# A planned DeltaNet and SwiGLU kernel: two early weight loads tied to the first solve, and a planner that replays a list of key changes

## The chip, the cores and the metric

The kernel runs on one core of one Trainium2 chip. The metric is the device time of one execution in microseconds; the median of the runs shown is what counts. A profiled execution is a single one; its span runs from its first to its last instruction.

## The reference

There are 4 batches of 8 heads, 768 tokens and head size 48, and a feed-forward of 384 to 1536 to 384 over 3072 tokens, all in float32 on the chip (the weights and inputs arrive as 64-bit numbers).

```python
k_n = k / (np.linalg.norm(k, axis=-1, keepdims=True) + 1e-06)
for t in range(S):
    y[:, :, t] = np.einsum('bhd,bhde->bhe', q[:, :, t], state)
    v_old = np.einsum('bhde,bhd->bhe', state, kt)
    state = state + bt[:, :, :, None] * np.einsum('bhd,bhe->bhde', kt, vt - v_old)
# x: y as (tokens, 384)
xn = x / rms * rms_g
g = xn @ w_gate
out = (silu(g) * (xn @ w_val)) @ w_out
```

## The kernel before

**The work.** The sequence is cut into 12 chunks of 64 tokens. For each chunk and head the recurrence over 64 tokens becomes a triangular system. The kernel computes the score matrix of the keys with themselves (`scores`, matmuls at L671), inverts a triangular matrix per head, applies the inverse to v minus the state's prediction, adds the part of the output that comes from within the chunk, and updates the state. The output of a chunk (4 batches x 64 tokens = 256 rows) is normalised, turned around, and goes through the feed-forward.

- Chunks 0 and 1 are solved by blocks of 16: `prep16` inverts the 16-blocks on DVE (L835, L841), and `recur` couples them by three rounds of small products (`couple`, L1202) with a subtraction on DVE (L1250) and copies on ACT (L1244) between the rounds. `first_rows` is L1190, the coupling matrices are L888 (copied by ACT at L893), the gather of the blocks is L780.
- Later chunks use blocks of 32: `prep` sends the scores through DRAM into another layout (`dkk`, `at`), inverts on DVE (L991, L997), sends the result back (`dx`, `dxt`, `m1bd`, `x2bd`, `mt`), and two merges on TensorE (`merge1` L1046 with its copy L1055, `merge2` L1066) fill the off-diagonal block. `recur` then does the products with the state (L1105), with the inverse (L1176), and L1212/L1284 for output and state.
- `norms` gives the key norms (L692 to L699), `qpart` the scores of q with k (L671, masked by DVE at L715), L1315 to L1370 the output's RMS and its transposition into `xf` or, for chunk 1, `xp1` (the profile's `xp`). ACT scales it with `g_sb` at L1370.
- The feed-forward of chunks 0 and 1 is plain (`ffn_plain`: up products L1433, ACT L1440, DVE L1441 writes `hf`, down products L1415), in two halves of the hidden width. The other ten use a fast product scheme with fewer multiplications (`ffn`: L1526, L1536, L1538, L1542, L1543, and `down`: L1583, L1575, L1588, L1592).
- `weights(n0, n1)` loads the feed-forward's weights in 18 pieces of 768 KB, numbered 0 to 17: gate, value, gate, value, out and so on. Each is converted from 64-bit numbers by ACT (L588) and four DVE operations (L576, L579, L584, L608). The buffers are three slices of `more`, but loads 3 and 4 use the two halves of `hf` (`early`), which the feed-forward doesn't use yet. All of these DMAs are issued by SP (L454).

**The order.** Nothing is scheduled by the compiler. Every step is given to a `Plan` with its engine, an estimated duration, a due time, and keys for what it reads and writes. `Plan.run` makes a list schedule (`forward`), takes the latest possible starts from it (`backward`) as the next keys, perturbs them a little, and repeats this 150 times; the plan with the earliest modelled end is emitted. Each engine executes its own list in that order, and waits on semaphores for what it reads. A step that SP, ACT or POOL waits for holds all that stands behind it on that engine. Where the plan has TensorE idle in the first 70 us, products with the identity matrix are put in as fillers (L1692). `RELEASE` gives the earliest planned time of each weight load; it puts no wait into the program.

The sequence in which steps are given to the plan (which fixes dependencies and the late steps' due times) is the loop at the end of the function: for each chunk `recur`, then the next chunk's `prep`, then the later weights, loads, norms and `qpart`, then the feed-forward.

Of the kernel before, what the change touches and what calls it, by code (L numbers as in the profile page):

```python
# [19 lines left out]
W = 32  # L20
# [5 lines left out]
ROUNDS, SEEDS = 150, (53,)  # L26
# [3 lines left out]
JKQ, JMR, JSC = 3, 99, 99  # L30
EARLYN = (3, 4)
RELEASE = (4.7, 10.0, 13.0, 16.0, 30.0, 33.0, 36.0)
# [39 lines left out]
class Plan:  # L72
# [198 lines left out]

    def run(self, free, filler=None, until=0.0):
        self.first_priorities()
        first = [op.key for op in self.ops]
        best = None
        self.ends = []
        for seed, k in itertools.product(SEEDS, range(ROUNDS)):
            if not k:
                rng = random.Random(seed)
                for op, key in zip(self.ops, first):  # L280
                    op.key = key
            order = self.forward([t for t, _ in free], until if filler else 0.0)
            if order is None:
                continue
            self.ends.append(self.end)
            if best is None or self.end < best[0]:
                best = self.end, [(op, op.start) for op in order]
            self.backward()
            for op in self.ops:
                if op.first:  # L290
                    op.key = op.n - 2000.0
                op.key += SHAKE * (k % 3) * rng.uniform(-1.0, 1.0)
        self.end = best[0]
        pe = 0.0
        free = list(free)
        for op, s in best[1]:
            op.start = s
            for g in op.acquire:
                if g.t is None:
                    g.t = free.pop(0)[1]  # L300
            if filler and op.eng == "PE":
                if s < until:
                    filler(fillers(pe, s))
                pe = s + op.dur
            op.fn()
            for g in op.release:
                g.left -= 1
                if not g.left:
                    free.append((s + op.dur + 0.1, g.t))
                    free.sort(key=lambda x: x[0])  # L310
# [3 lines left out]
def kernel(  # L314
# [298 lines left out]


# [46 lines left out]

    def scores(kt_, rhs, pr, r, w):

        ps = [Group(), Group()]

        def sc():
            for u in range(8):
                for d in range(2):
                    for g in range(2):
                        s, c_ = slice(64 * d, 64 * d + 64), slice(64 * g, 64 * g + 64)  # L670
                        nc.tensor.matmul(ps[d].t[c_, 64 * u : 64 * u + 64], kt_[s, u, c_], rhs[s, u, c_])  # L671

        P.rows = 64
        P.add("PE", 0.99, sc, pr, r=r, w=ps + w, ps=ps, size=128)
        P.rows = 128
        return ps
# [26 lines left out]
    def qpart(c):  # L703
        pr = (13.0, 41.0)[c] if c < 2 else due(c, 50)
        i2 = c % NKQ
        qk = [("qt", hv) for hv in range(2)]
        if c < 2:
            turn(q2, qt, qk, q2k + ["q2p"], pr, False)
        else:
            square_turn(qt, qk, pr)  # L710
        ptall = [("pt", d) for d in range(2)]
        ps = scores(kt[i2], qt, pr, qk + [("kt", i2, hv) for hv in range(2)], ptall)
        for d in range(2):
            dst = pt[:, d:16:2]
            P.add("DVE", 0.72, lambda d=d, dst=dst: nc.vector.tensor_tensor(  # L715
                out=dst, in0=heads(ps[d]), in1=mask_p[:, None, :].to_broadcast([128, 8, C]), op=ALU.mult,
            ), pr, r=[ps[d], "mask"], w=[("pt", d)], last=ps[d])
# [15 lines left out]
    def prep16(c):  # L733
# [147 lines left out]
        for h in range(2):  # L881
            ps = Group()

            def coupling(h=h, ps=ps):
                for z_ in range(8):
                    for g in range(2):
                        rows, x_ = slice(64 * g, 64 * g + 64), 8 * (z_ // 4) + 4 * h + z_ % 4
                        nc.tensor.matmul(ps.t[rows, 64 * z_ : 64 * z_ + 64], under[rows, x_], dg[c][rows, 8 * h + z_])  # L888

            P.rows = 64  # L890
            P.add("PE", 1.04, coupling, pi, r=[("dg", c, h), "under"] + (kkall if c else mtkeys()), w=[ps, ("ET", h)], ps=ps, size=64)
            P.rows = 128
            P.add("ACT", A(512), lambda h=h, ps=ps: nc.scalar.copy(et[:, 8 * h : 8 * h + 8], ps.t.rearrange("p (z t) -> p z t", t=C)), pi, r=[ps], w=[("ET", h)], last=ps)  # L893

    def prep(c):
        pr = due(c, 110)
        pn = due(c, 125)
        pd = pr + 1
        pi = due(c, 80)
        i2, ikq, ikk = c % 2, c % NKQ, c % 2  # L900
        kn = k2[c % NK]
        kd = kn[:, :, 0:D]
        kkeys = kkeys_(c)
        ktk = [("kt", ikq, hv) for hv in range(2)]

        fast = c < 4
        eng, e_ = (nc.vector, "DVE") if fast else (nc.gpsimd, "POOL")
        kkd = lambda d: [("kka", ikk // 2, d), ("kkb", ikk, d)]
        kkall = kkd(0) + kkd(1)
        kp = [("k2p", c % NK)]  # L910
        P.add("POOL", 1.6, lambda: nc.gpsimd.tensor_tensor(
            out=kd, in0=kd, in1=krec[i2][:, :, None].to_broadcast([128, 16, D]), op=ALU.mult,
        ), pn, r=[("krec", i2)], w=kkeys)
        if c < KSQ:
            turn(kn, kt[ikq], ktk, kkeys + kp, pr, False)
        else:
            dma(dsq, kn.rearrange("p x e -> p (x e)"), pn, r=kkeys + kp, w=["dsq"], dur=0.6, work=1.4)
# [5 lines left out]
        ps = scores(kt[ikq], kt[ikq], pr, ktk, kkall)  # L923
        for d in range(2):
            dst = kk[ikk][:, :, d:16:2]
            src = lambda d=d, ps=ps: ps[d].t.rearrange("p (u i t) -> p i u t", u=8, i=2)
            P.add("ACT", A(512), lambda dst=dst, f=src: nc.scalar.mul(dst, f(), -1.0), pr, r=[ps[d]], w=kkd(d), last=ps[d])

        dk = dkk[c % 2]
        for g in range(2):  # L930
            for i in range(2):
                r0 = 64 * g + W * i
                src = kk[ikk][r0 : r0 + W, i]
                kbkeys = [(("kka", ikk // 2, d), ("kkb", ikk, d))[i] for d in range(2)]
                dma(dk[i, g].rearrange("x j t -> j x t"), src, pd, r=kbkeys, w=[("dkk", c % 2, g, i)], work=0.5, dur=0.55)
# [105 lines left out]
        ps1 = Group()  # L1041

        def merge1():
            for b in range(B):
                for y_ in range(4):
                    nc.tensor.matmul(  # L1046
                        ps1.t[W * y_ : W * y_ + W, 64 * b : 64 * b + 64],
                        kk[ikk][:, 1, 4 * b + y_],
                        m1bd[:, 4 * b + y_].rearrange("p g s -> p (g s)"),
                    )  # L1050

        P.rows = 32
        P.add("PE", 0.5, merge1, pi, r=[("kkb", ikk, d) for d in range(2)] + [("m1bd", g, bb) for g in range(2) for bb in range(2)], w=[ps1, ("yn", 0)], ps=ps1, size=64)
        P.rows = 128
# [4 lines left out]
        ps2 = Group()  # L1059

        def merge2():
            for p in range(2):
                for g in range(2):
                    for bb in range(2):
                        r0 = 64 * bb + W * g
                        nc.tensor.matmul(  # L1066
                            ps2.t[r0 : r0 + W, 128 * p : 128 * p + 128],
                            zz[:, 2 * bb + p, g],
                            x2bd[:, 4 * g + 2 * bb + p].rearrange("p y t -> p (y t)"),
                        )  # L1070

        P.rows = 32
        P.add("PE", 0.5, merge2, pi, r=[("yn", 0)] + [("x2bd", y_) for y_ in range(4)], w=[ps2] + [("mt", 0, 2, bb, g) for bb in range(2) for g in range(2)], ps=ps2, size=32)
        P.rows = 128
# [6 lines left out]


    def recur(c):
# [11 lines left out]
        if c:  # L1095
# [26 lines left out]
            if c == 1:  # L1122
                scale_v(c, pr)
            P.rows = 64
            if c < JKQ:
                P.add("PE", 0.98, lambda: (on_state if c > 1 else on_state_rows)(kt[ikq], psk), pr, r=ktk + sk, w=psk + rk, ps=psk, size=128)
            else:

                def both_states():
                    on_state(kt[ikq], psk)  # L1130
                    on_state(qt, psq)

                P.add("PE", 1.96, both_states, pr, r=ktk + qk + sk, w=psk + psq + rk, ps=psk + psq, size=256)
# [118 lines left out]
        for h in halves:  # L1252
            gu = groups(psu, h) if c else [psu[0, h[0]]]
            P.rows = 64
            if c > 1:
# [5 lines left out]
            if c > 1:  # L1261
                continue
            ek = [("ET", p) for p in h]
# [372 lines left out]
    weights(0, 9)  # L1636
# [9 lines left out]
    for c in range(NCH):  # L1646
        for part_ in (recur, prep):
            P.late = c + (part_ is prep) > 1
            if part_ is prep:
                P.slack, P.lead = 0.0 if c < 1 else 0.2, 1000.0  # L1650
                if c + 1 < NCH:
                    (prep if c else prep16)(c + 1)
            else:
                P.slack, P.lead, P.first = 0.0 if c < 1 else 0.1, 1000.0, c == 0
                recur(c)
                P.first = False
# [5 lines left out]
        if c + 2 < NCH:  # L1662
            load(c + 2, "k")
            norms(c + 2)
# [63 lines left out]
```

## Time and profile before

| | us |
|---|---|
| Median of 3 runs (lowest, highest) | 676.82 (675.74, 678.0) |
| Profiled execution | 677.15 |
| Its span | 675.4 |
| TensorE busy | 660.1 |
| VectorE (DVE) busy | 547.8 |
| ScalarE (ACT) busy | 300.5 |
| GpSimd (POOL) busy | 133.6 |

The profile's page names engines as PE (TensorE's matmuls), PEld (its weight loads), DVE, ACT, POOL and SP. A line such as L1526 is the line of the kernel before. [...] "Idle before" with an arrow is the time that an engine sat idle ahead of an instruction, and what released it. The granted clock is the share of full speed that TensorE was given: its mean over the span is 0.995.

### The profile page before, as it was taken

To read this page: it belongs to the slowest core of one execution; us is meant where nothing else is said; L and a number is where in the kernel's file an instruction comes from. 1 tells how busy PE (TensorE), PEld (TensorE's weight loads), DVE (VectorE), ACT (ScalarE), POOL (GpSimd) and SP (SyncE) were. 2 spreads that over 40 slices of the span, in tenths; PEclk is the share of its full clock that TensorE was granted. 3 is DMA by queue.
4 is the path that set the end of the run, shared out by engine and by line. 5 is a ranking of instruction groups with operands and counts; after the bars stand their busy time and mean duration, and the time that the engine had idled before them with its cause. 6 is when DMAs were issued, how large, how long until landed. Compare 5 with 4: busy or idle time off the path is not lost.

```text
span 675.4 us, 23509 instructions
## 1 busy us (share of the span) xinstructions
PE 660.1 (98%) x10068; PEld 611.6 (91%) x10068; DVE 547.8 (81%) x1154; ACT 300.5 (44%) x693; POOL 133.6 (20%) x141
## 2 busy tenths in 40 slices
PE   8899999999999999999999999999999999999997
PEld 6787877778899999999999999999989999999997
DVE  6989999999699599599699599599699689467472
ACT  7565462244256355354444453454354354353341
POOL 4112031030321330331421331330331111000000
PEclk9989999999999999999999999999999999999999
DMA  9868985516114535445455635546535622402101
GB/s 141 257 110 197 240 197 109 91 26 107 36 34 71 89 77 94 77 97 92 69 138 74 115 94 85 104 106 100 90 76 104 113 48 58 72 2 48 24 1 24
DMA packets 266329, 62.32 MB, mean 92 GB/s; under 512 B 253168, under 2 KB 258288, under 8 KB 266224
## 3 DMA queue, kind: packets, MB, share of 16 engines
q1 hardware_dynamic: 263104, 60.22, 46.1%
q8 instruction: 79, 1.29, 0.8%
q10 hardware_dynamic: 3120, 0.59, 0.7%
q14 instruction: 26, 0.21, 0.1%
HBM read 44.25 MB, written 16.52 MB: 90 GB/s over the span
## 4 chain that ended last, share of the span: by engine, by line
PE 63%; DVE 15%; SPq 8%; DMA 7%; issue 3%; ACT 2%; POOL 1%; DVEq 0%; POOLq 0%; ACTq 0%
PE bank L1526 30%; PE bank L1583 16%; SPq L454 8%; PE bank L1433 5%; PE bank L1415 3%; DVE acc L997 2%; DMA more<-in_moe_w_val_dram 2%; DVE tmp L1536 2%; PE bank L1105 2%; DVE acc L991 2%; PE bank L671 2%; PE bank L1202 1%; DMA q<-dsq 1%; PE bank L1176 1%; PE bank L1212 1%
## 5 line engine op out<-in xcount | busy, mean ns | idle before, releaser
L1526 PE MATMUL bank<-xf,w_in 128*128 128x128 f32 x1440 | 181.0, 277 | 0.1
L1526 PEld LDWEIGHTS bank<-xf,w_in 128*128 128x128 f32 x1440 | 170.0, 192 | 3.2 <-issue 1.0
L1536 DVE TENSOR_TENSOR tmp<-tmp,bank 128x512 f32<-128x512 f32 x180 | 120.5, 680 | 39.6 <-PE bank L1526 27.3
L1526 PE MATMUL bank<-xf,more 128*128 128x128 f32 x960 | 124.2, 277 | 0.7 <-DVE tmp L1536 0.5
L1526 PEld LDWEIGHTS bank<-xf,more 128*128 128x128 f32 x960 | 114.9, 192 | 2.9 <-DVE tmp L1536 1.4
L1538 ACT COPY tmp<-bank 128x512 f32<-128x512 f32 x120 | 69.0, 585 | 78.3 <-PE bank L1526 62.4
L1542 ACT ACTIVATE tmp<-tmp 128x256 f32<-128x256 f32 x120 | 49.9, 418 | 100.0 <-DVE tmp L1536 99.9
L997 DVE TENSOR_REDUCE acc<-acc 128x30 f32<-128x90 f32 (+4 forms) x150 | 70.9, 473 | 5.2
L695 POOL TENSOR_TENSOR knrm<-ksum,half 128x16 f32<-128x16 f32 x12 | 35.7, 2979 | 152.7 <-DVE ksum L694 152.7
L1583 PE MATMUL bank<-wo_sb,hf 128*128 128x192 f32 x360 | 64.5, 329 | 0.0
L1583 PEld LDWEIGHTS bank<-wo_sb,hf 128*128 128x128 f32 x360 | 58.2, 190 | 0.7 <-issue 0.2
L991 DVE TENSOR_TENSOR acc<-acc,at 128x60 f32<-128x60 f32 (+4 forms) x150 | 51.3, 342 | 8.6 <-POOL at L974 3.3
L1543 DVE TENSOR_TENSOR hf<-tmp 128x256 f32<-128x256 f32 x120 | 50.2, 436 | 5.9 <-ACT tmp L1542 5.3
L944 POOL TENSOR_TENSOR at<-at,beta_b 128x1024 f32<-128x1024 f32 x8 | 18.9, 2358 | 129.7 <-DMA at<-dkk 99.3
L1017 POOL COPY acc<-acc 128x128 f32<-128x128 f32 x40 | 17.6, 469 | 91.5 <-DVE acc L997 91.1
L1415 PE MATMUL bank<-wo_sb,hf 128*128 128x384 f32 x96 | 34.0, 489 | 0.8 <-DVE hf L1441 0.8
L1433 PE MATMUL bank<-xf,w_in 128*128 128x256 f32 x144 | 34.6, 386 | 0.0
L1592 DVE TENSOR_TENSOR tmp<-tmp,bank 128x192 f32<-128x192 f32 x30 | 10.5, 350 | 28.5 <-PE bank L1583 28.5
L1433 PE MATMUL bank<-xp,w_in 128*128 128x256 f32 x144 | 32.8, 380 | 0.4 <-DVE hf L1441 0.4
L1433 PEld LDWEIGHTS bank<-xp,w_in 128*128 128x128 f32 x144 | 27.0, 190 | 5.4 <-DVE hf L1441 0.6
L1433 PEld LDWEIGHTS bank<-xf,w_in 128*128 128x128 f32 x144 | 26.5, 190 | 5.0
L1588 ACT COPY tmp<-bank 128x192 f32<-128x192 f32 x30 | 9.6, 321 | 42.8 <-PE bank L1583 38.4
(192 smaller groups left out, 1021.0 us busy)
## 6 DMA issues: line engine op xcount, KB each, us to landing
at<-dkk SPq DMA_DIRECT2D x20, 256.0 KB, 3.9
more<-in_moe_w_gate_dram SPq DMA_DIRECT2D x6, 768.0 KB, 9.6
vt<-in_v_dram SPq DMA_DIRECT2D x24, 192.0 KB, 4.6
out_dram<-tmp SPq DMA_DIRECT2D x48, 96.0 KB, 2.2
k<-in_k_dram SPq DMA_DIRECT2D x23, 192.0 KB, 3.9
more<-in_moe_w_val_dram SPq DMA_DIRECT2D x5, 768.0 KB, 6.2
more<-in_moe_w_out_dram SPq DMA_DIRECT2D x5, 768.0 KB, 5.7
dyn<-yn SPq DMA_DIRECT2D x16, 192.0 KB, 1.9
```

The costliest lines, as they stand in the source:

```text
L454: op = P.add(eng, dur, lambda: queue.dma_start(out=dst, in_=src), prio, r, w, lat=0.7)
L695: P.add("POOL", 2.95, lambda: nc.gpsimd.tensor_tensor(out=knrm[i2], in0=ksum[i2], in1=half, op=ALU.pow), pn, r=[("ksum", i2), "half"], w=[ ...
L991: nc.vector.tensor_tensor(out=acc[:, 1:3, 0:n, j + 2 : W].rearrange("p a i t -> p i a t"), in0=acc[:, old, 0:n, j : j + 2, None].to_broadc ...
L997: nc.vector.tensor_reduce(out=acc[:, new, 0:n, j + 2 : W], in_=acc[:, lo : lo + 3, 0:n, j + 2 : W].rearrange("p a i t -> p i t a"), axis=A ...
L1415: nc.tensor.matmul(po[p].t[:, 0:DM], hf[:, spot(f), 128 * p : 128 * p + 128], wo_sb[:, spot(f)], start=(f == f0), stop=(f == f1 - 1), skip ...
L1433: nc.tensor.matmul(ps.t[:, TOK * side : TOK * side + TOK], w_in[:, side, h_, 3 * t + i_, n : n + 128], x_[:, 2 * t : 2 * t + 2].rearrange( ...
L1526: nc.tensor.matmul(g.t[:, 128 * z : 128 * z + 128], fac[:, side, 128 * f : 128 * f + 128], xf[:, xs], start=(begin and z == 0), stop=False ...
L1536: P.add("DVE", V(512), lambda t=t, g=g: nc.vector.tensor_tensor(out=t, in0=t, in1=g.t, op=ALU.add), -1, r=[g], w=[tk], last=g)
L1538: P.add("ACT", A(512), lambda t=t, g=g: nc.scalar.copy(t, g.t), -1, r=[g], w=[tk], last=g)
L1542: P.add("ACT", A(256), lambda t=t: nc.scalar.activation(out=t[:, 0:256], in_=t[:, 0:256], func=ACTF.Silu), -1, w=[tk])
L1543: P.add("DVE", V(256), lambda t=t, f0=f0, p=p: nc.vector.tensor_tensor(out=hf[:, spot(f0) : spot(f0) + 2, 128 * p : 128 * p + 128], in0=t[ ...
L1583: nc.tensor.matmul(g.t[:, 0:192], a_[:, f], b_[:, f], start=(begin and f == 0), stop=(f == 5), skip_group_check=True)
```

## The change

- **Holds.** A new helper `hold(i, ...)` adds a one-element POOL copy into half `i` of `hf`. Loads 3 and 4 go into these halves, so that each now waits for its copy. The first copy reads the second coupling matrix of chunk 0 after ACT wrote it (L893); the second reads `u` of the second half of chunk 0 after ACT's copy (L1244). The loads 0 to 2 are given to the plan first; loads 3 to 8 after `recur(0)`. `RELEASE` gets one more 16.0 in place of 36.0.
- **Planner.** 150 rounds with seed 53 become 3 rounds with seed 23, followed by 61 listed seeds. Each seed stands for one draw in `shake`: it adds random amounts to the keys of some steps (1, 4 or 20% of those whose start lies in a stretch), or starts from `backward` anew. The earliest modelled end is kept, as before.
- **Stages.** `prep` is split into `kscores` (scores, their copy and the way to DRAM) and `invert`. `merge1` is given to the plan in `qpart`, ahead of the scores of q, and `merge2` in `recur`. Further branches, which would join merges and scores with other products into one step, are behind `JQM`, `JTM` and `JMK`; all three are 99, and with 12 chunks none of them is taken.

No other operation is added or removed, and no size changes. The core of the diff:

```diff
-ROUNDS, SEEDS = 150, (53,)
+ROUNDS, MOVES = (3, 23), (3000241, 3001356,
...
-RELEASE = (4.7, 10.0, 13.0, 16.0, 30.0, 33.0, 36.0)
+RELEASE = (4.7, 10.0, 13.0, 16.0, 16.0, 30.0, 33.0)
...
+    def shake(self, state):
+        def draw():
+            nonlocal state
+            state = (state * 6364136223846793005 + 1442695040888963407) % 2**64
+            return (state >> 11) * 2.0**-53
+        for _ in range(4):
+            draw()
+        kind, a, b, c = draw(), draw(), draw(), draw()
+        if kind < 0.03:
+            self.backward()
+            self.reorder()
+            for op in self.ops:
+                op.key += 0.24 * a * (draw() * 2.0 - 1.0)
+            return
+        share = 0.01 if a < 0.33 else 0.04 if a < 0.66 else 0.2
+        far = 0.5 if b < 0.33 else 2.0 if b < 0.66 else 6.0
+        wide = 2000.0 if kind < 0.4 else 30.0 if kind < 0.7 else 8.0
+        t = -1000.0 if kind < 0.4 else c * self.end
+        for op in self.ops:
+            x = draw()
+            if t <= op.start < t + wide and x < share:
+                op.key += far * (draw() * 2.0 - 1.0)
...
+        seed, rounds = ROUNDS
+        for k in range(rounds + len(MOVES)):
...
+            if k >= rounds - 1:
+                if k < rounds + len(MOVES) - 1:
+                    self.shake(MOVES[k - rounds + 1])
+                continue
             self.backward()
+            self.reorder()
...
+    def hold(i, src, keys):
+        first, P.first = P.first, False
+        P.add("POOL", 0.15, lambda: nc.gpsimd.tensor_copy(out=hf[:, 6 * i, 0:1], in_=src), 0, r=keys, w=[("hf", f, p_) for f in range(6 * i, 6 * i + 6) for p_ in range(2)])
+        P.first = first
...
+        if c < JQM:
+            if c > 1:
+                merge1(c)
+            ps = scores(kt[i2], qt, pr, qk + [("kt", i2, hv) for hv in range(2)], ptall)
...
+            if c == 0 and h:
+                hold(0, et[:, 8, 0:1], [("ET", 1)])
...
             if c == 1:
                 scale_v(c, pr)
+            elif c < JTM:
+                merge2(c)
...
+            if c == 0 and h[0]:
+                hold(1, u_[:, 4, 0:1], uk(h))
...
-    weights(0, 9)
+    weights(0, 3)
...
+        recur(c)
+        P.first = False
+        if c == 0:
+            P.lead = 0.0
+            weights(3, 9)
...
+        if c == 0:
+            prep16(1)
+        elif c + 1 < NCH:
+            if c < JMK:
+                kscores(c + 1)
+            invert(c + 1)
```

## The prediction

> **What bounds the kernel now.** I read the page's shares and slices first, then the busy time by stretches, then TensorE's instructions in order of time, then the chain of waits.
>
> ```profile
> PE 660.1 (98%) x10068; PEld 611.6 (91%) x10068; DVE 547.8 (81%) x1154; ACT 300.5 (44%) x693; POOL 133.6 (20%) x141
> PE   8899999999999999999999999999999999999997
> DVE  6989999999699599599699599599699689467472
> PEclk9989999999999999999999999999999999999999
> ```
>
> TensorE (PE) is busy in 98% of the span. But PE's busy time up to about 54 us holds filler products (L1692), and "busy" hides slow ones.
>
> ```profile
> 0.00:30.00 30.00, 25.38 (x512) 20.08 (x514) 22.83 (x67) 19.47 (x34) 9.74 (x17) 1.00 0.90 194
> 30.00:70.00 40.00, 38.42 (x758) 32.81 (x755) 37.09 (x73) 22.94 (x54) 6.49 (x4) 0.91 0.81 169
> 70.00:112.00 42.00, 40.10 (x725) 31.83 (x721) 40.55 (x79) 17.57 (x38) 8.43 (x8) 1.00 0.73 174
> 112.00:200.00 88.00, 88.00 (x1023) 72.91 (x1026) 79.24 (x160) 32.64 (x78) 16.57 (x14) 1.00 0.38 70
> ```
>
> The columns are PE, PEld, DVE, ACT, POOL, the granted clock, the DMA share and GB/s. From 112 us on PE has no slack: over 112 to 671.4 us it is busy 556.2 of 559.4 us, idle 3.2. From 30 to 112 us DVE is nearly full (77.6 of 82). So the end is PE's fixed work, plus what PE loses at the start, plus array switches, plus a 4.0 us tail (the span is 675.4, PE ends at 671.4).
>
> What PE loses at the start:
>
> ```profile
> 26.97 0.26 PE L763 MATMUL bank<-sel,krd 128*32 128x16 f32 x8
> 28.93 2.24 PE L1202 MATMUL bank<-u,wsum 64*64 64x48 f32 x64 [1.70 <-ACT u L1244]
> 31.39 6.63 PE L1202 MATMUL bank<-state,wsum 64*64 64x48 f32 x125 [0.22 <-ACT u L1244]
> ...
> 52.65 1.25 PE L1692 MATMUL bank<-ident 128*128 128x512 f32 x4
> 53.82 1.15 PE L1116 MATMUL bank<-state,kt 48*64 48x48 f32 x64
> 55.74 1.53 PE L1415 MATMUL bank<-wo_sb,hf 128*128 128x384 f32 x4 [0.77 <-DVE hf L1441]
> ```
>
> ```profile
> 31.00:32.00 1.00, 0.78 (x16) 0.62 (x15) 0.97 (x4) 0.34 (x1) 0.00 (x0) 0.50 0.66 162
> 32.00:37.00 5.00, 5.00 (x100) 5.00 (x97) 3.65 (x12) 0.68 (x2) 0.00 (x0) 0.50 0.44 131
> 37.00:38.00 1.00, 1.00 (x38) 1.00 (x40) 0.90 (x4) 0.28 (x1) 0.00 (x0) 0.75 0.00 0
> ```
>
> The first solve (L1202) runs at a granted clock of 0.50. In chunk 1 the same x64 group takes 2.07 us, so 128 records need 4.1; here they take 6.6. This follows a hole of 1.70 us in PE's work. The last filler and the first down product (L1415) cost 1.17 + 0.77 us more.
>
> **The change part by part.** Both programs as built hold the same instructions on PE, DVE, ACT and SP, but for fillers (48 units of 128 columns become 43) and two one-element copies on POOL. The tail's orders on PE, DVE and ACT are the same. All else is order.
>
> *Array switches, -2.1 us.* After the first up product of chunk 1 (L1433 on xp), PE's queue changes between 128-row and smaller products 132 times before and 118 after: seven round trips fewer (merge 1 moves beside the scores, for one). Their price:
>
> ```profile
> 137.07 1.29 PE bank L1433 x6
> 138.37 1.08 PE bank L1176 x64
> 139.44 1.49 PE bank L1433 x6
> 140.94 1.29 PE bank L1415 x4
> ```
>
> The same six take 1.29 us on their own and 1.49 after a small group; the small group itself is some 0.1 longer than inside a pair (0.97). 7 x 0.3 = 2.1; the lower bound is 7 x 0.2 = 1.4.
>
> *First solve, -2.2 us (0 to -2.5).* In the new orders PE runs chunk 1's gather (L780) where a filler stood, so both L888 follow at once (the second ends near 24.0, was 25.0), and L1202 may start near 27.5 instead of 28.93. That alone gains nothing: DVE reaches the first change (L1250) near 30.4, against 30.22, since the same conversions stand ahead of it. From there at full clock: L1250 0.5, ACT's copy 0.5, L1202 1.03 for each half, two rounds: L1212 near 36.4 instead of 38.66. This supposes that the clock is not halved.
>
> *The first down product, -1.9 us.* DVE's L1441 now stands ahead of the conversion of load 5 (L576, L579, L584: 52.05 to 54.1) and of L693/L694 (1.1), so 3.1 us sooner beside the shift. PE has no filler after chunk 1's L868: 1.17 + 0.77 go. What is late next is the chain of chunk 1: in the new order one up group and one down product stand between its steps, where DVE's and ACT's queues took 1.1 us too long before (L1212 at 80.56).
>
> *New waits, +1.5 us.* DVE stays full from 30 to 112 us and gives PE its work in another order. The bounds are 0 and +3.2 (PE's whole idle time after 112 us, once more); I take 1.5, near the 1.1 + 0.3 that PE lost at 80.56 and 92.61.
>
> *The holds, 0.* The trace has no such copy: between 0.10 (POOL's 128x1 memset) and 0.55 us (its L1334), in a POOL idle for 15.4 us until 39.60; behind them stands only L1334. SP stops at load 3 until the second coupling is copied (near 26.4) and at load 4 until u is copied (near 28.5), where it issued them at 16.93 and 17.86. Behind them wait v of chunk 1, load 5 and g (30.23 becomes some 31.5). With the longest landing of the early loads, 9.6 us, load 4 lands at 38.1, before its use after 42; g would land at 41.1, against L1370 near 40.8: 0.3 us at most.
>
> Do the held loads slow loads 1 and 2? Load 1 was issued at 15.69 and landed 8.3 us later, load 2 at 16.40 and 9.6 later: 24.0 and 26.0, one after the other. The Trainium skill (DMA: Bandwidth & Descriptors, Queues, rings and completion order) says that each DMA engine takes descriptors in ring order; by that rule the hold can't bring them forward, and this trace agrees. Had the four shared the bandwidth, ACT's 4.6 us wait for load 1 would shrink by about 2 and the sum would be near 670.1.
>
> The sum: -2.1 - 2.2 - 1.9 + 1.5 = -4.7. The profiled execution took 677.15 us (span 675.4 and 1.75 around it), 0.33 above the median of 676.82. 677.15 - 4.7 - 0.33 = **672.1 us**.
>
> **The rivals.** (1) *The half clock stays.* PE's holes move but don't vanish: some 1.6 us before L1202, and 1.6 more before the first change. The first-solve term is 0: 674.3. For it: 1.70 us of idle was enough at 30.7. Against: the holes are no longer and may fall across two stretches. The Trainium skill (TensorE: Matmul & The Clock Gate, Part 1) gives about 3.4 us of an idle window before the clock halves; this trace halved after a hole of 1.70 beside others under 1, so the measurement decides; by the rule this rival would have no chance.
>
> (2) *The inverse comes late*, the one that can end slower. From the scores of a chunk (L671) to the last landing of mt before L1176 the trace shows 77.2, 73.5, 70.7, 77.3, 76.4 and 73.3 us for chunks 4 to 9. The new PE order leaves, by summed rows, 77.5, 76.2, 73.4, 74.3, 74.6 and 74.9. PE waits in order. At the old latencies 3.0 + 1.8 = 4.8 us come back: 676.9, no change. If all took 77.5 it would be 14.1 us: 686.2, slower. It decides from 6.7 us of such waits. Against it: chunk 6 made it in 70.7, and these transfers often waited behind others on SP.
>
> (3) *Better still*: no new waits, and half of the 3.2 us of idle time goes: 669.0.
>
> **How the numbers follow.** Forecast 672.1: 0.45. Half clock 674.3: 0.20. Inverse at old latencies 676.9: 0.12; later still, slower: 0.06. Better, 669.0: 0.17. The range 669.0 to 677.0 leaves out the late inverse and the edges. 0.3% (2.0 us) is about what a measurement can tell from no change, so faster is below 674.8: the forecast, the better case and three quarters of the half-clock case, 0.77. Same 0.16, slower 0.07.
>
> **What would show it.** Granted clock 1.00 between 27 and 40 us and L1212 of chunk 0 near 36.4; no L1692 after chunk 1's L868; L1415 first near 51 (was 55.74); the first up on xp near 91 (was 93.54); 14 fewer switches; PE's idle after 112 us at 3 to 5 us. Wrong, if PE waits ahead of L1046 or L1176, or the clock falls to 0.50 again.

## The result, and the profile after

The changed kernel is slower, by 0.5%. Its median over 12 runs is 678.77 us (676.65 to 683.94), that of the kernel before, over the 12 runs beside them, 676.91 us (675.53 to 680.4). The ratio is 1.0051, with a 95% interval of 1.0026 to 1.0075. The forecast was 672.1 us and the range ended at 677.0.

The planner's first part is 23 rounds from seed 3, where the section on the change has 3 rounds with seed 23. The 61 listed seeds follow as told there.

The profiled execution of the changed kernel took 683.94 us, span 682.2. It is the longest of the 12; a second profile of the same kernel (run 1) shows the same, smaller. The mean granted clock of the 12 runs goes with their times: 0.990 in four (median 682.5 us), 0.992 in three (680.4), 0.995 in three (677.8) and 0.997 in two (676.7). In the lines of the changed kernel L1537 is the old L1433, L1519 the old L1415, L1545 the old L1441, L1291 the old L1202, L1301 the old L1212, L1489 the old L1385, L1805 the filler. POOL's three steps of the inverse are L1007 (scale; was L944), L1032 (first share; was L969) and L1037 (second share; was L974).

Its page first: busy times, then the slices.

```profile
PE 660.4 (97%) x10062; PEld 611.0 (90%) x10062; DVE 564.0 (83%) x1154; ACT 299.6 (44%) x693; POOL 138.6 (20%) x143
...
PE   8799989999899999999999999989999999999997
...
DVE  6889999999799898698899898599699689457473
...
PEclk9989999999899899999999999999999999999999
```

TensorE (PE) works as long as before, DVE 16 us longer with the same 1154 instructions. The granted clock now dips at three places instead of one: slice 3 as before, and slices 11 and 14. Next the busy time by stretches (PE, PEld, DVE, ACT, POOL, clock, DMA share, GB/s), the same stretches as before and the long one to the end:

```profile
30.00:70.00 40.00, 37.06 (x696) 31.79 (x700) 36.45 (x75) 21.98 (x53) 6.16 (x4) 0.91 0.83 182
70.00:112.00 42.00, 38.61 (x753) 31.15 (x746) 39.22 (x72) 17.05 (x36) 5.97 (x4) 1.00 0.80 188
112.00:200.00 88.00, 85.21 (x970) 67.86 (x969) 81.44 (x160) 32.69 (x78) 21.43 (x19) 0.98 0.38 69
...
112.00:677.80 565.80, 558.60 (x8092) 527.52 (x8091) 466.42 (x946) 241.76 (x573) 116.31 (x116) 0.99 0.41 74
```

From 112 us on PE is idle for 7.2 us where it was 3.2, and its clock is no longer full throughout. The first solve, by PE's instructions in order of time, is what it was:

```profile
27.17 2.14 PE L1291 MATMUL bank<-u,wsum 64*64 64x48 f32 x64 [0.65 <-ACT u L1333]
29.25 0.26 PE L813 MATMUL bank<-sel,krd 128*32 128x16 f32 x8
31.40 6.74 PE L1291 MATMUL bank<-state,wsum 64*64 64x48 f32 x126 [1.89 <-ACT u L1333]
37.92 0.26 PE L1301 MATMUL bank<-u,pt 64*64 64x48 f32 x2
...
54.13 1.53 PE L1519 MATMUL bank<-wo_sb,hf 128*128 128x384 f32 x4 [1.36 <-DVE hf L1545]
```

The hole moved from ahead of the first L1291 to ahead of the second, and the 6.7 us at half clock stayed.

What is new stands at 168 us. The lines are of the engines' instructions in order of time (start, duration, engine and line):

```profile
163.13 0.74 DVE L1545 TENSOR_TENSOR hf<-tmp,bank 128x256 f32<-128x256 f32 x2
...
168.17 2.91 DVE L1489 TENSOR_TENSOR xf<-xf 128x256 f32<-128x256 f32 x2
168.17 2.62 POOL L1007 TENSOR_TENSOR at<-at,beta_b 128x1024 f32<-128x1024 f32 x1 [12.23 <-DMA x2bd<-dx]
...
170.87 1.79 POOL L1032 TENSOR_TENSOR acc<-at 128x512 f32<-128x512 f32 x1
171.00 2.20 DVE L1595 TENSOR_TENSOR more<-w_in 128x512 f32<-128x512 f32 x1
173.13 0.41 DVE L1545 TENSOR_TENSOR hf<-tmp,bank 128x256 f32<-128x256 f32 x1
...
173.59 2.29 PE L1537 MATMUL bank<-xp,w_in 128*128 128x256 f32 x6 [2.79 <-DVE hf L1545]
```

Two sums of DVE (L1489), 0.4 us each elsewhere, take 2.91 us beside POOL's scale; the next step (L1595), 0.68 us elsewhere, takes 2.20 beside POOL's first share. Behind them in DVE's queue stands the L1545 that PE waits for: PE has a hole of 2.79 us. In the single records the first sum takes its 0.42 us, the second starts at 168.50 and ends 0.28 us after the scale does. That fits a step that stood still until POOL was done, and not one that ran slower throughout. The Trainium skill (SBUF — State Buffer, Who interferes with whom) says just this of a DVE instruction with two SBUF inputs and a POOL instruction that reads SBUF: they share a port, and the second one stands until the first is through. The trace agrees.

The kernel before has the same POOL steps. There they fall where DVE waits for PE, or reads PSUM:

```profile
171.68 0.42 DVE L1441 TENSOR_TENSOR hf<-tmp,bank 128x256 f32<-128x256 f32 x1 [0.15 <-ACT tmp L1440]
...
172.33 2.36 POOL L944 TENSOR_TENSOR at<-at,beta_b 128x1024 f32<-128x1024 f32 x1 [19.05 <-DMA at<-dkk]
...
174.76 1.73 POOL L969 TENSOR_TENSOR acc<-at 128x512 f32<-128x512 f32 x1
...
176.67 0.55 DVE L1407 TENSOR_TENSOR tmp<-tmp,bank 128x384 f32<-128x384 f32 x1 [4.57 <-PE bank L1415]
...
176.98 1.29 POOL L974 TENSOR_TENSOR at<-at,acc 128x512 f32<-128x512 f32 x1
```

The hole is then paid a second time. In stretches of 3.41 us around it and around a second hole (PE waits 1.29 us for DVE's L765 at 231.81, behind five sums that took 5.46 us):

```profile
170.86:174.28 3.42, 0.69 (x3) 0.64 (x4) 3.42 (x5) 0.36 (x1) 3.33 (x4) 1.00 0.25 39
174.28:177.69 3.41, 3.41 (x9) 2.06 (x7) 3.17 (x11) 0.00 (x0) 0.60 (x1) 0.50 0.48 90
228.89:232.30 3.41, 2.12 (x116) 1.80 (x112) 3.41 (x5) 1.69 (x5) 3.25 (x5) 1.00 0.46 56
232.30:235.72 3.42, 3.42 (x50) 3.33 (x42) 2.44 (x7) 0.86 (x2) 0.54 (x1) 0.50 0.31 35
```

PE is busy for 0.69 and 2.12 us of the first and the third stretch, and the one behind each is at clock 0.50. In 3.41 us at half clock PE does the work of 1.7, so each costs about 1.7 us more.

How an order that the planner took for 6.2 us shorter (its own end is 666.40 us, against 672.65 for the order before) became longer is seen by setting each PE step's planned start against its start in the trace. The lag, as the median over 20 us of plan:

```
planned time     40    80   160   220   440   660
kernel before   1.2   1.3   0.8   0.3   1.3   0.3
changed         2.4   5.5   9.2  12.0  14.7  13.4
```

The plan of the kernel before comes true. The changed one loses 2 us at the first solve and 3 near 80 us; 2.0 of these 3 are a hole at 87.5 us that waits for nothing the profile shows, and that run 1 doesn't have. It loses 4.4 and 3.0 in single steps at 170 and 230 us, each beside POOL's steps of one chunk. DVE stands still beside POOL's steps near 287, 335 and 382 us too, without a step in PE's lag. Near 440 us 2.6 us are lost in several small steps, and there no DVE step stands still: POOL's first share lasts 2.53 instead of 1.76 us beside a DVE step (L1679), and DVE then waits 3.42 us for POOL's last step.

### The profile page after: what moved, and what is told of

Its sections match the earlier page's. It is cut to its first block, busy times and chain, and to the rows that moved or that the text cites. A ratio compares the mean times of both kernels' runs of the same rounds, so it can differ in the third digit from the quotient of the medians.

```text
span 682.2 us, 23510 instructions
## 1 busy us (share of the span) xinstructions
PE 660.4 (97%) x10062; PEld 611.0 (90%) x10062; DVE 564.0 (83%) x1154; ACT 299.6 (44%) x693; POOL 138.6 (20%) x143
## 3 DMA queue, kind: packets, MB, share of 16 engines
q8 instruction: 79, 1.29, 0.8%
## 4 chain that ended last, share of the span: by engine, by line
PE 60%; DVE 20%; SPq 6%; DMA 6%; issue 3%; POOL 3%; ACT 1%; DVEq 0%; POOLq 0%; ACTq 0%
PE bank L1630 31%; PE bank L1687 15%; SPq L485 6%; DVE acc L1060 4%; DVE tmp L1640 3%; DVE acc L1054 3%; PE bank L704 2%; PE bank L1519 2%; PE bank L1291 2%; PE bank L1537 2%; PE bank L1183 1%; PE bank L1301 1%; DMA more<-in_moe_w_val_dram 1%; DMA at<-dkk 1%; PE bank L1265 1%
## 5 line engine op out<-in xcount | busy, mean ns | idle before, releaser
L1054 DVE TENSOR_TENSOR acc<-acc,at 128x60 f32<-128x60 f32 (+4 forms) x150 | 52.1, 348 | 14.3 <-POOL at L1037 12.4
L1647 DVE TENSOR_TENSOR hf<-tmp 128x256 f32<-128x256 f32 x120 | 48.4, 421 | 6.8 <-ACT tmp L1646 6.2
L1007 POOL TENSOR_TENSOR at<-at,beta_b 128x1024 f32<-128x1024 f32 x8 | 19.6, 2454 | 136.1 <-DMA at<-dkk 67.6
L1080 POOL COPY acc<-acc 128x128 f32<-128x128 f32 x40 | 19.3, 513 | 96.5 <-DVE acc L1060 95.9
L1489 DVE TENSOR_TENSOR xf<-xf 128x256 f32<-128x256 f32 (+1 forms) x70 | 35.7, 547 | 3.0 <-ACT xf L1463 2.4
L1519 PE MATMUL bank<-wo_sb,hf 128*128 128x384 f32 x96 | 36.4, 508 | 1.4 <-DVE hf L1545 1.4
L1537 PE MATMUL bank<-xp,w_in 128*128 128x256 f32 x144 | 33.7, 388 | 2.8 <-DVE hf L1545 2.8
L1537 PEld LDWEIGHTS bank<-xp,w_in 128*128 128x128 f32 x144 | 27.2, 192 | 7.6 <-DVE hf L1545 3.2
L1537 PE MATMUL bank<-xf,w_in 128*128 128x256 f32 x144 | 33.8, 384 | 0.0
L1537 PEld LDWEIGHTS bank<-xf,w_in 128*128 128x128 f32 x144 | 26.7, 190 | 4.6
```

Source lines behind the costliest of these rows:

```text
L1054: nc.vector.tensor_tensor(out=acc[:, 1:3, 0:n, j + 2 : W].rearrange("p a i t -> p i a t"), in0=acc[:, old, 0:n, j : j + 2, None].to_broadc ...
L1519: nc.tensor.matmul(po[p].t[:, 0:DM], hf[:, spot(f), 128 * p : 128 * p + 128], wo_sb[:, spot(f)], start=(f == f0), stop=(f == f1 - 1), skip ...
L1537: nc.tensor.matmul(ps.t[:, TOK * side : TOK * side + TOK], w_in[:, side, h_, 3 * t + i_, n : n + 128], x_[:, 2 * t : 2 * t + 2].rearrange( ...
L1647: P.add("DVE", V(256), lambda t=t, f0=f0, p=p: nc.vector.tensor_tensor(out=hf[:, spot(f0) : spot(f0) + 2, 128 * p : 128 * p + 128], in0=t[ ...
```

## The experiments

**Theory A**: POOL's steps of the inverse now fall beside DVE steps that work on SBUF alone, these stand still, PE runs dry, and a hole brings a stretch of half clock. **Theory B**: the held loads cost the time. **Theory C**: the new order (or the new stages) is no better by itself; the saved switches are worth nothing. Each group of runs had its own runs of the kernel before beside it (medians 674.12 to 675.88 us by chip), so ratios are compared.

**1. The changed kernel again.** No edit.

> The changed kernel once more, nothing edited, for a second profile. Theory A (late POOL steps: the three POOL steps of the inverse, L1007, L1032 and L1037, fall beside DVE steps that read and write SBUF alone, these then last as long as POOL's, PE runs dry, and a hole of PE is followed by a stretch of granted clock 0.50) expects a median of 677 to 680 us, and in each profile the same count of extra half-clock stretches as of holes over 1.2 us that fill one stretch of 3.41 us. Theory B (the two held loads) expects the same time, and the lost time before 60 us. Theory C (the new order is no better by itself, the seven saved switches are worth nothing) expects the same time with the lost time spread over all chunks.

Measured: 677.69 us (11 runs, 675.51 to 683.21), ratio 1.0062 (1.0036 to 1.0087). Its profile has the same holes at the same places (3.3 us for L1545 of the same product, 1.3 for L765), one further stretch of half clock at 171.9, and lags of 1.8, 2.8, 7.5, 8.7, 10.1 and 9.3 us at the six times above: steps at the same places as theory A has it, not a spread over all chunks. B's "before 60 us" is out. The two holes are the same in both profiles, but A's count of half-clock stretches isn't: the hole of 1.3 us was followed by one in the first profile and not in this one.

**2. The holds away.** In `hold`:

```diff
-P.add("POOL", 0.15, lambda: nc.gpsimd.tensor_copy(out=hf[:, 6 * i, 0:1], in_=src), 0,
+P.add("POOL", 0.15, lambda: None, 0,
```

> The changed kernel with both one-element copies left out, the planned order of every other instruction kept, so that loads 3 and 4 go out as soon as SP reaches them. Theory A and theory C: within 1 us of the changed kernel (678.8). Theory B: at or below the kernel before, 674 to 676.5.

Measured: 680.78 us (5 runs), ratio 1.0094 (1.0074 to 1.0115). Theory B falls: without the holds the kernel is no faster. Whether it is slower the intervals, which overlap, don't settle.

**3 and 4. POOL's steps cut short, in both kernels.** For chunks 4 to 11 `n_` is 1 in the three steps:

```diff
-eng.tensor_tensor(out=at_, in0=at_, ...)
+eng.tensor_tensor(out=at_[:, 0:n_], in0=at_[:, 0:n_], ...)
```

> The changed kernel in its own order, with POOL's three steps of the inverse (L1007, L1032, L1037) of chunks 4 to 11 cut to one of 32 columns: most of the scaling and sharing of these chunks is left out. Theory A: DVE's xf sums (L1489) go back from 547 to about 390 ns, no half clock after 40 us, PE's holes at 173 and 231 us go, and the time is 671.5 to 674.5. Theory C: within 1.5 us of 678.8, since PE's order is the same. Theory B: the same as C.

> The same cut in the kernel before (its L944, L969 and L974): the same scaling and sharing is left out. Theory A: DVE loses little beside POOL there (0.8 us at most at one step), so 675.5 to 677, within 1.5 us of the kernel before. If the POOL steps bound both kernels by their length alone, this kernel falls by as much as the changed one, to 670 to 673.

Measured: the changed kernel falls to 667.14 us (ratio 0.9894, 0.9873 to 0.9916), the kernel before stays at 674.73 (1.0003, 0.9987 to 1.002). What PE waited for longest in the cut changed kernel (total, times, longest):

```profile
PE bank L1391 <- issue: 2.5, 2, 1.6
PE bank L1808 <- POOL ident masks.py:199: 1.4, 1, 1.4
PE bank L1304 <- DVE u L1338: 1.0, 1, 1.0
```

No wait for hf is among them, there is no half clock between 42 and 660 us, and the xf sums (here L1492) are back at their old length:

```profile
L1492 DVE TENSOR_TENSOR xf<-xf 128x256 f32<-128x256 f32 (+1 forms) x70 | 24.4, 386 | 3.0 <-ACT xf L1466 2.4
```

Behind the bar stand their total in us and their mean in ns: 386 here, 547 in the changed kernel, 383 before. Theory C falls for this order: without the collision it is 7.6 us shorter than the old one (667.14 against 674.73, same chip), and 4.4 us under A's range of 671.5 to 674.5. The cut takes away POOL's length as well as the collision; runs 5, 9 and 10 change them separately.

**5. POOL takes its turn.** All work is done; ahead of each scale POOL copies one element that DVE's last planned step wrote:

```diff
+            if getattr(op, "turn", False):
+                self.take_turn()   # gpsimd.tensor_copy(out=turn_sb, in_=one element of that step's output)
             op.fn()
```

> The changed kernel in its own order, with a one-element copy on POOL ahead of each of the eight scale steps (L1007 of the changed kernel) of chunks 4 to 11; it reads what DVE's last step planned ahead of that scale writes, so POOL can't begin before DVE is through. Nothing is left out. Theory A (POOL begins while DVE still has steps on SBUF alone that the plan puts ahead of it; those then wait for POOL): 667 to 671 us, no wait of PE for hf at 170 us, DVE's xf sums (L1489) near 390 ns, no half clock between 40 and 660 us. Its rival (the POOL steps cost by their length: the inverse comes late through them, whatever DVE does): 678 or more, since POOL now begins later still.

Measured: 674.99 us (12 runs), ratio 0.9984 (0.9964 to 1.0005). The hole at 170 us is gone, and the lag there is 2.6 us instead of 9.2. But the time is 4 us above A's range, and the sums (L1489) take 447 ns, not 390: the turn cures only DVE steps that POOL overtook. Those that come while POOL's three steps are still running stand still as before. DVE was lengthened beside POOL by 12.6 us (19.4 in the changed kernel, 5.3 before), and waited 17.3 us for POOL's result instead of 12.4.

**6. PE kept warm at the first solve.** Two fillers ahead of the second L1291:

```diff
+                if c == 0 and not h[0] and n == 1:
+                    op.warm = [4, 2]
```

> The changed kernel with two more filler products (512 and 256 columns) in PE's hole of 1.89 us ahead of the first L1291 that reads state, all else as it is. The prediction's first-solve step (at full clock L1301 of chunk 0 begins near 36.4 instead of 37.9, worth up to 2.2 us): no stretch of 0.50 between 27 and 40 us, and 1.5 to 2.2 us less than the changed kernel in the same runs (677.7 on the last chip). Its rival (DVE and ACT set the pace of the rounds, or the time won is lost again before chunk 1 ends): within 0.7 us of the changed kernel.

Measured: 677.19 us (12 runs), ratio 1.0026 (0.9996 to 1.0055), against 1.0062 and 1.0051 for the changed kernel. No half clock between 27 and 40 us, and the lag at 40 us is 0.2 instead of 2.4. By the ratios that is 1.7 to 2.4 us, but the intervals overlap; run 12 tries the fillers a second time.

**7 and 8. Less search.** `MOVES` cut to its first 20 entries; then `ROUNDS, MOVES = (53, 150), ()`.

> The changed kernel with only the first 20 of its 61 key changes: the planner's own end for this order is 672.42 us, against 672.65 for the kernel before and 666.40 for the changed one. Theory A (each further key change buys planned time by putting POOL's steps edge to edge with DVE's): 673.5 to 677, close to the kernel before, with DVE less delayed beside POOL than the 19 us of the changed kernel. Theory C (the stages and holds cost the time, not the search): as slow as the changed kernel, 678 or more.

> The changed program (stages emitted separately, holds, new release times) with the search of the kernel before (150 rounds from seed 53, no key changes). Its planned end is 675.01 us, 2.36 above the kernel before. Theory A: the plan comes true within 2 us, so 676 to 679. Theory C: the stages or holds cost over 2 us beside that, 680 or more.

Measured: 680.07 us (1.0063, 1.0034 to 1.0093) and 679.10 us (1.0058, 1.003 to 1.0087). The first misses A's numbers: this order, planned as long as that of the kernel before, is as slow as the changed one. Its DVE is lengthened beside POOL by 18.9 us, so it isn't only the late key changes that bring the collision. But that it costs the time here isn't shown. PE's longest hole in the profile of this run stands behind steps of chunk 3, which DVE does itself, and a stretch of half clock follows it at 126.3 us:

```profile
122.88 1.22 DVE L1007 TENSOR_TENSOR at<-at,beta_b 128x1024 f32<-128x1024 f32 x1
124.13 1.12 DVE L1032 TENSOR_TENSOR acc<-at 128x512 f32<-128x512 f32 x1
...
125.64 2.32 PE L1519 MATMUL bank<-wo_sb,hf 128*128 128x384 f32 x4 [2.76 <-DVE hf L1545]
```

PE's lag behind this plan is between 1.2 and 3.5 us at the six times, in an execution of 677.81 us, below the median. So standing still on DVE need not cost PE much, and why this order is slow stays open. The second kernel came out near A's numbers (676 to 679): its plan is 2.4 us longer than that of the kernel before and comes true (PE is between 2.5 us ahead of it and 0.4 behind), although DVE loses 11.3 us.

**9. POOL's steps in four pieces.**

```diff
-eng.tensor_tensor(out=at_, in0=at_, ...)
+for z in range(0, W, n_):   # n_ = W // 4
+    eng.tensor_tensor(out=at_[:, z : z + n_], in0=at_[:, z : z + n_], ...)
```

> The changed kernel in its own order, with POOL's scale (L1007) and both shares (L1032, L1037) of chunks 4 to 11 cut into four pieces of 8 columns each; all of the work is done, still on POOL. Theory A (a DVE step on SBUF alone waits for the end of the POOL instruction that runs beside it): DVE now waits for a quarter, so its xf sums fall from 547 to about 430 ns and the time to 670 to 675, though POOL's steps last as long in all. Its rival (the length of POOL's steps costs, not what they block): 677 to 680, as the changed kernel or slower by the further instructions.

Measured: 674.52 us (12 runs), ratio 1.0012 (0.999 to 1.0035). The sums (L1495 here) take 462 ns, where A had 430. POOL's steps are longer in all than in the changed kernel, and still the kernel is faster:

```profile
165.23 3.59 POOL L1009 TENSOR_TENSOR at<-at,beta_b 128x256 f32<-128x256 f32 x4 [11.53 <-DMA x2bd<-dx]
168.90 2.51 POOL L1036 TENSOR_TENSOR acc<-at 128x128 f32<-128x128 f32 x4
```

3.59 and 2.51 us here, 2.62 and 1.79 in one piece; PE's hole ahead of the same product is 1.69 us instead of 2.79. So POOL's length alone isn't what costs: it also matters for how long one POOL instruction holds DVE up. What DVE's waits for POOL's result add (12.4 us in the changed kernel, 10.3 here, none in run 10) these runs don't separate.

**10 and 11. POOL's steps given to DVE**, at their planned places, in both kernels:

```diff
-eng, e_ = (nc.vector, "DVE") if fast else (nc.gpsimd, "POOL")
+eng, e_ = nc.vector, "DVE" if fast else "POOL"
```

> The changed kernel with these POOL steps of chunks 4 to 11 given to DVE, at the place in the order where the plan had them on POOL; the plan itself is unchanged, and nothing is left out. They take 1.27, 1.17, 0.30 and 0.69 us there by the planner's costs for chunks 2 and 3, 3.4 per chunk instead of some 6 on POOL. Theory A: no step runs beside POOL's any more, DVE has 100 us of idle time to take 27 us, and the time falls to 669 to 674, near the kernel with the cut POOL steps (667.1). Its rival (DVE has no room where they fall): 677 or more, with PE waiting for DVE at more places.

> The same in the kernel before: the POOL steps of chunks 4 to 11 on DVE, at their planned places. Theory A: nothing to win there, since POOL's steps hardly meet DVE's in that order; 27 us more work on DVE: 675 to 678, from 1 us under to 2 us over the kernel before. Its rival (the steps are better on DVE in any order): it gains as much as the changed kernel does by the same edit.

Measured: 669.74 us (6 runs), ratio 0.9925 (0.9898 to 0.9953), for the changed kernel; 674.02 us, ratio 0.9992 (0.997 to 1.0013), for the one before. The first is inside A's range. The second is 0.1 us under the kernel before, inside the band that A had around it, though under its 675 to 678. The page of the changed one:

```profile
PE 655.5 (98%) x10062; PEld 607.1 (91%) x10062; DVE 575.0 (86%) x1194; ACT 299.9 (45%) x693; POOL 87.4 (13%) x103
```

By the planner's costs DVE has some 27 us more to do, and it is busy only 11 longer than in the changed kernel, since 14 us of standing still are gone. Its steps at the same place, in order of time:

```profile
165.95 0.76 DVE L1489 TENSOR_TENSOR xf<-xf 128x256 f32<-128x256 f32 x2
167.22 1.22 DVE L1007 TENSOR_TENSOR at<-at,beta_b 128x1024 f32<-128x1024 f32 x1
168.36 0.41 DVE L1545 TENSOR_TENSOR hf<-tmp,bank 128x256 f32<-128x256 f32 x1
```

The scale takes 1.22 us there instead of 2.62, and PE's hole ahead of the same product (168.83 us) is 0.74 us instead of 2.79. PE's lag behind the plan is 1.3, 2.5, 2.7, 2.4, 2.3 and 0.1 us at the six times: the plan comes true.

**12. Both repairs**: experiment 10 with the fillers of experiment 6.

> Both repairs in the changed kernel: the POOL steps of chunks 4 to 11 on DVE, and two filler products in PE's hole of the first solve. If both mechanisms add up, 1.5 to 2.2 us less than the changed kernel with the steps on DVE alone, near 668, and no stretch of half clock; this would be under both kernels. If the time won at the start is lost in a later wait, the same as with the steps on DVE alone.

Measured: 668.04 us (6 runs, 667.67 to 669.59), ratio 0.9907 (0.9885 to 0.9929). Of the kernels that do all of the work it has the lowest median, and it is clearly below the changed kernel and the one before. The medians put the fillers at 1.7 us (669.74 to 668.04), as in run 6; the intervals overlap here too, so two experiments agree on the sign and the size is rough. The first solve in it:

```profile
28.94 1.56 PE L1809 MATMUL bank<-ident 128*128 128x512 f32 x4
30.91 4.16 PE L1293 MATMUL bank<-state,wsum 64*64 64x48 f32 x125 [0.41 <-ACT u L1335]
34.85 0.25 PE L1303 MATMUL bank<-u,pt 64*64 64x48 f32 x1
```

The rounds take 4.16 us instead of 6.74 in the changed kernel, and their end comes at 34.85 instead of 37.92. In the profile of run 10, where only one stretch of 3.41 us was at half clock, it came at 36.37.

All together, with the time that DVE's steps lasted beyond the usual (the lower quartile of their form) while POOL ran, from each profile:

| kernel | planned end | median us | ratio to before | DVE lengthened beside POOL |
|---|---|---|---|---|
| before | 672.65 | 674.1 to 676.9 | 1 | 5.3 |
| before, steps on DVE | 672.65 | 674.02 | 0.9992 | 4.4 |
| changed | 666.40 | 678.77 and 677.69 | 1.0051 and 1.0062 | 19.4 and 18.9 |
| changed, first 20 key changes | 672.42 | 680.07 | 1.0063 | 18.9 |
| changed, old search | 675.01 | 679.10 | 1.0058 | 11.3 |
| changed, steps in four | 666.40 | 674.52 | 1.0012 | 15.6 |
| changed, turn taken | 666.40 | 674.99 | 0.9984 | 12.6 |
| changed, fillers alone | 666.40 | 677.19 | 1.0026 | 17.3 |
| changed, steps on DVE | 666.40 | 669.74 | 0.9925 | 5.1 |
| changed, both repairs | 666.40 | 668.04 | 0.9907 | 5.0 |

The last column counts all of POOL's steps; some 5 us of it stand beside steps other than the inverse's in every kernel. Beside the inverse's alone it is 0.6 us before, 14.5 and 14.1 in the changed kernel, 14.9 with the first 20 key changes, 6.2 with the old search, 10.7 in four pieces and 7.0 with the turn.

## Why the prediction was wrong

**The step that failed is "New waits, +1.5 us", with bounds 0 and +3.2.** It took the price of the new waits from the waits that the old order had. The runs put 8.5 to 9.2 us in its place: the changed kernel is at 1.0051 and 1.0062, the same order with the steps on DVE at 0.9925, a difference of 1.3 to 1.4% of 675. Part of this is half clock: at the same mean clock of 0.994 to 0.995 the changed kernel is about 1.6 us over the kernel before (three runs, run 1) and the one with the steps on DVE about 3.4 under it (two runs, run 10). So about 5 us are left without it, roughly, from so few runs. PE's idle time after 112 us, foreseen at 3 to 5 us, was 7.2, and two stretches of half clock came on top. The term named no mechanism; it should have asked which DVE steps stand beside which POOL steps in the new order. The old trace showed the danger only by its absence: 21 of the 24 long steps of POOL there lay beside an idle DVE or one that reads PSUM, and at the other three neither engine lost more than 0.7 us. In the changed kernel 12 of the 24 meet a DVE step on SBUF alone. The planner does keep such steps apart, but only in its own time. It planned the two sums of 168 us for 163.00 and 163.34 and POOL's scale for 164.36, the very moment when DVE's last step on SBUF ends. No wait in the program binds the two. DVE's two sums came 5.2 us late behind a late PE, POOL's scale, which a transfer released, 3.8 us, and the second sum fell inside the scale.

**First solve, -2.2: it did not come; the first rival did.** L1301 starts at 37.92 (37.80 before). The hole of 1.89 us moved, and the clock was halved at 30.92, where it had been at 30.67. Runs 6 and 12 put the price of the term at 1.7 to 2.4 us, with overlapping intervals; L1301 then comes at 34.85, sooner than the 36.4 that the prediction had at full clock. Nothing in the new order filled the hole, so the chance of 0.20 for this rival looks low afterwards.

**Array switches, -2.1 (at least -1.4): about right.** From the first L1212 or L1301 to the last product PE has the same 9386 or 9387 records in all kernels (two records to nearly every product). Their time without fillers and holes (each record until the next starts) is 621.94 us in experiment 11 and 620.72 in 10, 622.39 in 4 and 619.58 in 3: 1.2 and 2.8 us less. With the two new half-clock stretches (3.4) taken off, the changed kernel's 624.92 against 622.92 (the kernel before) gives 1.4 less. This is the time of all records; that the saved switches are what shortens it isn't shown apart.

**First down product, -1.9: mis-sized.** It comes at 54.13 instead of 55.74, where 51 was foreseen; with a full clock at the first solve it comes at 51.63 (run 12). Fillers behind the first solve fall by 1.0 us (4.3 to 3.3), but one of 1.14 us still stands behind chunk 1's L918 (the old L868) at 43.37, where the prediction had none, and the hole ahead of the product grew from 0.77 to 1.36. About -0.4 is left of it. The first up product on xp, foreseen near 91 us, comes at 96.78, and at 94.04 in run 1 (93.54 before).

**Holds, 0: right** (run 2). Loads 3 and 4 go out at 25.93 and 28.45 us in the changed kernel, where 26.4 and 28.5 were foreseen, and loads 1 and 2 land at 23.98 and 25.87, as before (23.98 and 26.01). **The inverse comes late (second rival): it did not.** PE waits at most 1.2 us for a transfer ahead of a merge in any profile, and 0.3 in the changed kernel's.

The sum of the parts, in ratios: without the collision and with part of the half clock the new order stands at 0.9925, where the forecast's 672.1 over 676.82 is 0.9930. A gain of the size that was forecast is there, and nearly twice as much is lost beside POOL. That the sizes agree is in part luck. By the profiles of runs 11 and 10 the new order is 3.8 us shorter with the steps on DVE in both: the first solve 0.9, the records 1.2, the fillers 1.1, the holes 0.6, where the forecast had 2.2 and 2.1 for the first two, 1.9 for the first down product, and 1.5 more for new waits. What stays open is why the new program's orders meet POOL's steps so much more than the old one's, which run 8 shows without any key change.

## What to carry to other kernels

Before trusting a new order of the same instructions, list for each long POOL step on SBUF which two-input DVE steps the order puts beside it, and allow for a slip of a few us between the queues: a planned gap of nothing can become a collision. Set planned starts against the trace's starts; a lag that grows in steps shows where to look, and a planner's gain is worth only what survives there. A step that stands still costs only where PE runs dry behind it. If DVE has room, doing the step on DVE itself is one cure: here some 27 us more of its work gave back about 9, and in the kernel before it cost nothing.

## What the chip showed beside this

- **The clock is judged in fixed stretches.** The half-clock stretches of the changed kernel begin at 30.92, 174.28 and 232.30 us: 42 and 59 times 3.413 us apart. Stretches on this grid with PE busy for 0.69, 1.74, 1.99 and 2.12 of 3.41 us were followed by half clock; one with 2.30 (78.46 in the kernel before) was not, nor were two of 2.05 and 1.96 in the changed kernel (51.40 and 85.53) and one of 1.72 in run 9 (167.94), so busy time alone doesn't decide. In run 1 the hole of 1.29 us ahead of L1183 lies across the border of two stretches, with PE busy for 2.32 us of the first, and no half clock follows. The Trainium skill (TensorE: Matmul & The Clock Gate, Part 1) has the window of 3413 ns that runs free, which agrees, and an idle window as the condition, which doesn't: a hole of 1.29 us was enough.
- **A hole in PE, with no wait.** PE stops after 53 of the 64 records of chunk 1's L1388 for 2.02 us in the changed kernel, for 0.90 with short POOL steps and for 0.30 with the steps on DVE; the second profile of the changed kernel (run 1) has no such hole. In the first, PE stops from 87.49 to 89.51 us, and a packet of 16,384 bytes on an instruction queue takes 1.33 us from 86.92 on. Whether a block of instructions came late there is not shown.
